# First loads of q and k cut by halves of 18-token rows, and a new order of all steps, in a fused window attention and expert attention kernel

## The chip, the cores and the metric

The kernel runs on one core of a Trainium2 chip. The core has a matrix engine (TensorE, PE in the profile), VectorE (DVE), ScalarE (ACT), GpSimd (POOL), and SyncE (SP), which here only issues transfers; 16 DMA engines move data between the memory of the chip (HBM) and the core's own memory. The metric is the time of one execution on the device, in microseconds (us); lower is better.

## The reference

Two layers follow each other. The first is attention over 576 tokens with a window of 32 to each side, for 8 batches and 8 heads of width 64. Its output, with the heads side by side, is the input of the second: four experts with causal attention, of which a gate picks two for each token.

```python
# first layer: q, k, v are (8, 8, 576, 64)
scores = (q @ k.T) / 8
scores = where(abs(i - j) <= 32, scores, -1e9)
x = softmax(scores) @ v                      # -> x: (8, 576, 512), heads side by side
# second layer
logits = x @ w_gate                          # 4 experts, the best 2 of each token
w = softmax(logits of the best 2)
for e in range(4):
    q, k, v = x @ wq[e], x @ wk[e], x @ wv[e]          # 64 wide
    ye = softmax(causal(q @ k.T / 8)) @ v @ wo[e]
    out += (w of expert e where chosen) * ye
```

## The kernel before

The whole kernel is a list of steps, `ORDER`, a long string. A loop at the end of the program goes through it and calls for each word the function of that name: the digits are arguments (the batch first), the digits behind `@` are banks of PSUM, the small memory into which TensorE writes, and a last letter `a`, `v` or `g` is the engine that does a copy or a mask (ScalarE, VectorE or GpSimd). Each engine works through its own instructions in the order in which the list issues them, and an instruction waits until its inputs have been written and its outputs are free. So the list alone sets what stands behind what on each engine, and one late instruction holds up all that is queued behind it on its engine.

For batch `b`, head group `g` (four heads each) and half `half` of the tokens, the steps are:

- `lq`, `lk`, `lv`: SP issues the loads of q, k and v. `load()` ties each to the last TensorE instruction that was issued before it in the list, so that loads don't run far ahead.
- `tq`, `tk` (function `turn`): VectorE turns q and k in blocks of 32 by 32, so that the head dimension lies on the partitions. A q or k tile holds 18 consecutive tokens of one head in each partition (4 heads by 32 partitions).
- `sc`: TensorE makes the scores of one half of the tokens; `ex`: ScalarE takes the exponential; `mk`: GpSimd, or in two cases VectorE, multiplies by the window's mask.
- `av`: TensorE multiplies by v and by a column of ones; `vc` copies parts of v to where `av` needs them; `un`: VectorE divides by the sums.
- `xt`, `xf`, `xb`: x is turned by TensorE, copied out of PSUM, and cast to bf16.
- `ga`, `gt`, `ge`, `gm`, `gu`: the gate and its top two.
- `pp`, `pe`, `pv`, `ve`, `ps`, `xe`, `se`, `po`, `oe`, `pt`, `ot`, `py`, `ye`, `st`: projections, causal attention of the experts, the output projection and the store, each product with the copy that takes it out of PSUM.
- `wl0` to `wl3` load the weights, `cw0` to `cw3` cast them to bf16. `s_pads` sets the padding of a dozen tiles to zero on VectorE, `s_ones` sets some ones, `s_mask` makes the mask on GpSimd, `s_warm` makes ScalarE load its table.

The q and k of batch 0 are loaded in halves, by steps of their own: `fk` (issued by SP) and `fq` (issued by ScalarE) call `first_load`, and `gk` and `gq` call `first_turn`. The half `x` of a head group is one range of tokens, so that each partition gets 9 (or 10 and 8) consecutive tokens of it, and the half of the scores that lies in that range can begin before the other half has been loaded. The source is written with the heads outermost: 4 heads, then 32 rows, then the elements of a row.

Of the kernel before, what the change touches and what calls it, by code (L numbers as in the profile page):

```python
# [20 lines left out]
HS = 288  # L21
# [8 lines left out]
    un03@6 un02@4 xt00@0 xt02@2 lv13 xt01@4 xf00@0v mk1001 mk1010 xb00@g cw1@v xf02@2a xf01@4a sc110@26  # L30
    xb02@g mk1011 xb01@v cw0@v lv14 lk21 sc111@04 ex1100@2 ex1110@0 ex1111@4 ga0@2 lv10 pp000@0 ex1101@6
    lv11 tq20 gt0@2 pp001@6 vc11@a ge0@2 pe000@0a gm0@2 gu0@2 tk20 pe001@6a pp011@4 pe011@4a lq31 pp010@0
    pe010@0a mk1000 mk1110 mk1111 ps002@4 xe002@4 ps000@2 wl2 av12@6 xe000@2 mk1100 mk1101 un12@6 av13@0
    ps003@4 vc10@g ps001@2 ps012@6 xe003@4 xe001@2 xe012@6 lq21 un13@0 av14@4 un14@4 xt11@0 wl3 xf11@0a
    ps013@4 ps010@2 av10@6 xe010@2 xe013@4 tk21 lq30 av11@0 un10@6 sc201@42 un11@0 lv23 ex2010@4 mk2010
    xt12@6 lk30 ex2011@2 xt10@0 cw2@v xf10@0a pv00@4 pv01@7 lv24 lv22 ve00@4a sc200@02 ex2000@0 se013 xb10@g
    se003 ex2001@2 lv33 xb11@g xf12@6v tq21 ve01@7v xb12@v se000 sc211@46 ex2111@6 mk2011 ex2110@4 mk2000
    se001 mk2001 ps011@0 xe011@0 pp111@2 pp100@6 pe111@2a lv32 sc210@04 ex2100@0 pe100@6a vc21@a lv21 lv20
    ga1@2 pv10@0 ex2101@4 lk31 ve10@0a po000@6 pp101@4 tq30 tk30 lq40 tq31 gt1@2 oe000@6 gm1@2 ge1@2
    pe101@4a pp110@0 pe110@0a cw3@a gu1@2 sc301@46 lv34 lq50 mk2110 se011 mk2111 mk2101 mk2100 av24@0  # L40
    ex3010@4 ex3011@6 av22@2 un24@0 ps112@0 ps100@6 un22@2 xe100@6 xe112@0 vc31@a vc20@g av23@4 un23@4
    av21@2 un21@2 lv41 lv31 av20@6 ps101@4 ps102@0 un20@6 xe101@4 xt21@2 xe102@0 xf21@2v se010 lv43 se101
    lv30 po010@6 xt22@4 xf22@4a xt20@0 xf20@0a xb22@v oe010@6 se100 xb21@g sc300@42 lk40 ga2@0 ex3000@4
    ex3001@2 tk31 xb20@g ps103@4 xe103@4 ps111@6 ps113@2 xe113@2 pt000@1 ot000@1v gt2@0 gm2@0 mk3011 xe111@6
    pv20@4 ge2@0 pt010@1 ot010@1v gu2@0 ve20@4a lv42 tq40 sc311@62 ex3110@6 ex3111@2 lk41 pp211@4 mk3010
    sc310@60 se113 mk3001 mk3000 pe211@4a ex3101@0 mk3110 se103 mk3101 ex3100@6 mk3100 mk3111 lv40 lq41
    pp201@4 py01@0 tk40 vc30@g pe201@4a pp200@6 pe200@6a sc401@42 ex4011@2 ex4010@4 lv44 ye01@0v st01
    sc400@60 ex4000@6 ex4001@0 tk41 av34@2 ps202@4 ps110@6 py02@3 xe202@4 xe110@6 av33@0 lk50 av31@4 un34@2
    pv11@2 ve11@2a vc40@g ye02@3a av30@6 tq41 un33@0 un31@4 un30@6 mk4000 mk4011 av32@0 un32@0 po100@4 lq51
    xt32@2 xt30@6 xf30@6a lq60 oe100@4 xf32@2v pp210@0 sc411@24 pe210@0a sc410@06 lk51 se111 tk50 vc41@g  # L50
    mk4010 se110 ex4110@2 ex4111@4 ps211@2 ex4100@0 xe211@2 ex4101@6 mk4110 tq50 xt31@4 py00@0 xf31@4v
    po110@2 oe110@2 ps212@4 ps213@6 ye00@0a xe213@6 xe212@4 mk4111 av43@0 se201 ps200@6 st00 xb32@g lv50
    un43@0 xb30@v xe200@6 ps201@2 st02 lv54 xe201@2 ga3@4 gt3@4 ge3@4 gm3@4 gu3@4 sc500@60 mk4100 mk4101
    mk4001 xb31@g av42@2 ex5001@0 ps210@0 ps203@4 un42@2 ex5000@6 lk60 xe203@4 xe210@0 pp300@6 pp301@2
    pt100@0 pt110@1 tk51 ot100@0v pe300@6a tq51 sc501@64 lk61 ot110@1a pe301@2a ex5010@6 ex5011@4 av44@0
    ps302@2 ps301@6 lq70 se210 mk5010 xe302@2 mk5011 se211 un44@0 pv31@1 se200 se203 mk5000 ve31@1a av40@4
    un40@4 py12@0 av41@2 pv21@1 un41@2 xe301@6 lv52 ye12@0a sc510@46 tk60 xt42@0 py10@2 ve21@1a ex5100@4
    ex5101@6 xf42@0v lv53 lv51 xt41@4 py11@6 ye10@2a se213 ye11@6v xf41@4a po210@2 xt40@4 xf40@4a pp310@6
    oe210@2 xb42@g ps303@2 xe303@2 pe310@6a ps300@0 st11 st10 po200@4 xb40@g xb41@v lv62 vc51@g xe300@0 lq61
    pt210@2 ot210@2v pp400@6 pe400@6v oe200@4 sc511@20 ex5111@0 ex5110@2 pp311@6 pe311@6v tq60 tq61 vc50@g  # L60
    se301 tk61 lv60 lv64 st12 lv63 mk5101 mk5111 mk5001 pp411@0 pt200@2 pe411@0a ot200@2a pp401@6 ps311@0
    pe401@6a ps312@4 pv30@2 xe311@0 xe312@4 sc601@06 ga4@4 ve30@2a ex6010@0 ex6011@6 ps400@0 ps403@2 mk5110
    mk5100 gt4@4 xe403@2 ps313@6 av54@5 xe313@6 vc61@g se303 lk70 sc600@62 ge4@4 xe400@0 gm4@4 gu4@4 un54@5
    av50@0 un50@0 ex6001@2 ex6000@6 ps310@2 ps402@4 av53@6 lv61 xe402@4 xe310@2 se403 se313 mk6000 se310
    un53@6 av52@0 un52@0 av51@4 py22@2 pv41@3 un51@4 ye22@2a ve41@3a sc610@06 sc611@24 ex6100@0 ex6101@6
    lv70 lk71 ex6111@4 ex6110@2 tq70 se300 xt50@0 py20@6 po300@2 xt51@4 mk6001 xf50@0a se311 tk70 py21@0
    xf51@4a oe300@2 ye20@6v mk6110 xb50@g mk6111 lq71 se401 pp410@2 pt300@4 xt52@5 st20 xf52@5a po310@6
    ot300@4v pv40@4 xb52@v oe310@6 ve40@4v xb51@g ye21@0a pe410@2a ps413@6 xe413@6 mk6011 ps412@2 ps401@0
    xe401@0 mk6010 se400 vc60@g xe412@2 se411 mk6100 mk6101 lv74 st21 pp510@6 pe510@6v tq71 pp501@4 pe501@4a
# [561 lines left out]
```

## Time and profile before

| | us |
|---|---|
| median of 3 runs | 280.54 |
| lowest and highest | 278.0 and 280.75 |
| the profiled execution | 280.03 |
| its span (first to last instruction) | 278.1 |
| TensorE busy | 221.1 |
| VectorE busy | 192.6 |
| ScalarE busy | 151.8 |
| GpSimd busy | 150.8 |

The profiled execution took 280.03 us, of which 278.14 us are the span that the trace covers; 1.9 us lie around it. It is 0.5 us under the median of the three runs. Busy times are sums over a program with different stages: each says how much of the span an engine worked, not which of them set the time at a given moment.

### The profile page before, as it was taken

The numbers are of one execution on the slowest core, as the hardware profiler recorded it, in microseconds if no ns is written. First come the engines' busy times: TensorE is split into PE (matmuls) and PEld (weight loads), VectorE is DVE, ScalarE is ACT, GpSimd is POOL, SyncE is SP. The second block draws the span as 40 slices with busy tenths as digits, with TensorE's granted clock in tenths as the row PEclk, the third lists the DMA queues.
The fourth block names the chain that finished last, engine by engine and source line by source line (L and its number), as shares of the span: only waits on it lengthen the run. The fifth ranks groups of instructions, "written<-read, shape, count | busy, mean of one in ns | idle before, by whom it ended". The sixth has DMA issues, their size and how long they took to land.

```text
span 278.1 us, 12345 instructions
## 1 busy us (share of the span) xinstructions
PE 221.1 (79%) x5536; PEld 178.7 (64%) x5536; DVE 192.6 (69%) x381; ACT 151.8 (55%) x234; POOL 150.8 (54%) x166
## 2 busy tenths in 40 slices
...
GB/s 54 156 126 105 203 192 173 173 115 229 157 277 114 209 181 172 130 220 158 246 166 175 177 248 168 90 86 169 167 60 42 123 89 2 2 172 10 146 173 189
DMA packets 55286, 40.65 MB, mean 146 GB/s; under 512 B 45249, under 2 KB 46273, under 8 KB 55233
## 3 DMA queue, kind: packets, MB, share of 16 engines
...
q10 hardware_dynamic: 608, 1.25, 1.3%
...
## 4 chain that ended last, share of the span: by engine, by line
PE 50%; DVE 25%; DMA 10%; issue 7%; ACT 4%; POOL 1%; SPq 1%; ACTq 0%; DVEq 0%; POOLq 0%
PE PS L170 43%; DMA kn<-in_k_dram 10%; PE PS L173 7%; DVE Tqn L287 5%; DVE Tkn L287 4%; DVE XTB L158 2%; DVE XN L380 2%; DVE OE L548 1%; DVE PS L446 1%; DVE ATE L212 1%; DMA out_dram<-Y 1%; DVE A L354 1%; ACT A L350 1%; ACT QKE L154 1%; DVE WQ L158 1%
## 5 line engine op out<-in xcount | busy, mean ns | idle before, releaser
L354 POOL TENSOR_TENSOR A<-A,MASKP 128x576 f32<-128x576 f32 x62 | 87.5, 1432 | 49.1 <-ACT A L350 49.1
L170 PE MATMUL PS<-Tqn,Tkn 32*64 32x128 f32 (+2 forms) x2560 | 50.3, 285 | 30.2 <-DVE Tqn L303 15.6
L170 PEld LDWEIGHTS PS<-Tqn,Tkn 32*64 32x64 f32 x2560 | 43.5, 146 | 37.0 <-DVE Tqn L303 15.7
L350 ACT ACTIVATE A<-PS 128x576 f32<-128x576 f32 x64 | 38.4, 650 | 47.0 <-PE PS L170 44.5
L520 ACT ACTIVATE ATE<-PS 128x1024 bf16<-128x1024 f32 (+1 forms) x64 | 50.9, 839 | 13.0 <-PE PS L170 12.3
L170 PE MATMUL PS<-V,A 128*64 128x65 f32 (+1 forms) x1280 | 42.7, 231 | 8.1 <-DMA V<-in_v_dram 3.7
L170 PEld LDWEIGHTS PS<-V,A 128*64 128x64 f32 (+1 forms) x1280 | 38.8, 139 | 12.6 <-DMA V<-in_v_dram 3.8
L527 POOL TENSOR_SCALAR_AFFINE_SELECT ATE<-ATE 128x512 bf16<-128x512 bf16 (+1 forms) x48 | 24.8, 531 | 34.2 <-ACT ATE L520 28.1
L287 DVE STREAM_TRANSPOSE Tqn<-qn 128x576 f32<-128x576 f32 x28 | 32.4, 1240 | 0.7 <-PE PS L170 0.7
L287 DVE STREAM_TRANSPOSE Tkn<-kn 128x576 f32<-128x576 f32 x28 | 32.5, 1238 | 0.0
L156 POOL CAST XTB<-XTF 128x1024 bf16<-128x1024 f32 (+1 forms) x20 | 14.8, 758 | 31.3 <-DVE XTF L158 21.6
L154 ACT COPY XTF<-PS 128x1024 f32<-128x1024 f32 (+1 forms) x18 | 13.4, 769 | 25.9 <-PE PS L173 25.7
L380 DVE TENSOR_TENSOR XN<-PS,RC 128x512 f32<-128x512 f32 x32 | 22.1, 692 | 1.2
L173 PE MATMUL PS<-ident,XN 128*128 128x128 f32 x144 | 21.0, 294 | 1.6 <-issue 1.2
L156 POOL COPY V<-V 64x1024 f32<-64x1024 f32 (+1 forms) x22 | 21.2, 963 | 1.3
L170 PE MATMUL PS<-WO,OTT 128*128 128x512 bf16 (+1 forms) x96 | 19.5, 346 | 2.2 <-ACT ATE L520 1.5
L170 PE MATMUL PS<-XTB,WQ 128*128 128x288 bf16 x128 | 18.6, 288 | 2.3 <-ACT QKE L154 2.3
L154 ACT CAST QKE<-PS 128x576 bf16<-128x576 f32 x24 | 15.1, 644 | 8.5 <-PE PS L170 8.5
L173 PEld LDWEIGHTS PS<-ident,XN 128*128 128x128 f32 x144 | 17.1, 150 | 3.8 <-issue 1.4
L170 PE MATMUL PS<-WV,XTB 128*128 128x256 bf16 (+1 forms) x192 | 18.6, 255 | 1.1 <-DVE XN L386 0.5
L170 PE MATMUL PS<-QKE 64*128 64x64 bf16 (+4 forms) x192 | 17.0, 283 | 1.5 <-DVE OE L548 1.2
L170 PEld LDWEIGHTS <-ATE 128*128 128x128 bf16 x480 | 16.5, 97 | 2.6 <-issue 1.1
...
## 6 DMA issues: line engine op xcount, KB each, us to landing
...
qn<-in_q_dram SPq DMA_DIRECT2D x14, 576.0 KB, 5.0
kn<-in_k_dram SPq DMA_DIRECT2D x14, 576.0 KB
...
```

The costliest lines, as they stand in the source:

```text
L154: nc.scalar.copy(o, i)
L156: nc.gpsimd.tensor_copy(o, i)
L158: nc.vector.tensor_copy(o, i)
L170: PACE[0] = nc.tensor.matmul(*args, **kw)
L173: PACE[0] = nc.tensor.transpose(*args)
L212: nc.vector.memset(t[:, 2048:3584], 0.0)
L287: nc.vector.transpose(T[:, dh, :].rearrange("q (p o) -> q o p", o=18), n_[:, :, 32 * dh:32 * dh + 32])
L350: nc.scalar.activation(a_part(b, g, half, p), two(b0)[:, :, 0:HS], EXP, scale=scale_att)
L354: (nc.gpsimd if eng == "g" else nc.vector).tensor_tensor(out=ap, in0=ap, in1=MASK[:, None, HS * half:HS * half + HS].to_broadcast([128, 2, ...
L380: nc.vector.tensor_tensor(out=XN[T // 2][:, T % 2, :].rearrange("p (g h d) -> p g h d", g=2, h=4), in0=u[:, :, :, 0:64], in1=rc[:, :, :, N ...
L520: nc.scalar.activation(A[:, at:at + 2 * step].rearrange("p (e x) -> p e x", e=2)[:, :, 0:w], two(b0)[:, :, 0:w], EXP, scale=scale_moe)
L527: nc.gpsimd.affine_select(ap, ap, pattern=[[0, n], [1, w]], compare_op=IS_GE, fill=0.0, base=64 * j if c == 3 else 0, channel_multiplier=-1)
```

## The change

Two things are changed. The first is how the q and k of batch 0 are loaded and turned. A half is now the first or the last 9 tokens of each row of 18, over all 128 rows of a head group, and the source is written with these 128 rows outermost. Every half thus holds tokens from the whole length, and both halves of q and of k of a group have to be turned before any scores of that group can begin. The second is the list: all its steps are the same in number and kind, but they stand in another order, with other banks and partly with another engine for a copy. The two long strings share no line; the first lines of each are shown.

```diff
 ORDER = """
-    s_mask fq00 gq00 fk10 fq10 s_ones gk10 fk11 fk00 gq10 s_warm fq11 fq01 lq10 fk01 gk00 sc010@02 lv02
-    sc000@46 ex0101@2 ex0000@4 ex0100@0 lv01 lk10 gk11 gq01 lv00 gk01 gq11 sc001@04 tq10 tk10 s_pads lv03
...
+    fk01 fq01 fk11 s_pads fk00 s_warm gq01 s_ones fq10 fq00 fq11 gk00 lv04 lv14 fk10 lv01 lk10 gk01 gq00
+    sc001@02 ex0010@0 ex0011@2 gk11 gq11 gq10 gk10 lv02 sc000@46 ex0000@4 ex0001@6 lq10 lv00 sc011@64 tk10
+    s_mask mk0001@g ex0111@4 tq10 lv03 sc010@20 ex0110@6 mk0011@g mk0110@g s_ident mk0111@v lk11 mk0010@v
...
-    FIRST = {"qn": ((0, 9), (9, 18)), "kn": ((0, 10), (10, 18))}
-
     def first_load(nm, src, q_, g, x):
-        o0, o1 = FIRST[nm][x]
         t = NAT[nm][g][:, :, :].rearrange("p o d -> p (o d)")
-        q_.dma_start(t[:, 64 * o0:64 * o1], src[0, 4 * g:4 * g + 4, 32 * o0:32 * o1].rearrange(
-            "h (p o) d -> h p (o d)", p=32))
+        q_.dma_start(t[:, HS * 2 * x:HS * 2 * (x + 1)],
+                     src[0, 4 * g:4 * g + 4].rearrange("h (p o) d -> (h p) (o d)", o=18)[:, HS * 2 * x:HS * 2 * (x + 1)])

     def first_turn(nm, g, x):
-        o0, o1 = FIRST[nm][x]
         for dh in range(2):
-            nc.vector.transpose(QKT[nm][g][:, dh, 32 * o0:32 * o1].rearrange("q (p o) -> q o p", p=32),
-                                NAT[nm][g][:, o0:o1, 32 * dh:32 * dh + 32])
+            nc.vector.transpose(QKT[nm][g][:, dh, :].rearrange("q (p o) -> q o p", o=18)[:, 9 * x:9 * x + 9, :],
+                                NAT[nm][g][:, 9 * x:9 * x + 9, 32 * dh:32 * dh + 32])
```

Over the whole list the copies change engines as follows: `cw` on ScalarE 1 before and 3 now; `pe` on ScalarE 24 and 18; the large `ve` on ScalarE 5 and 7, the small one 6 and 3; the large `xf` on ScalarE 12 and 14, the small one 3 and 6; the large `xb` on GpSimd 12 and 8 (the others on VectorE); the large `ye` on ScalarE 11 and 13, the small one 8 and 5.

SP's queue at the start of the program, before. `kn` and `qn` are the k and q tiles as loaded, `V` the v tiles; 128x1x640 is a half of 128 rows with 640 elements each.

```order
L297 DMA kn_69<-in_k_dram 128x1x640
L297 DMA kn_69<-in_k_dram 128x1x512
L297 DMA kn_68<-in_k_dram 128x1x640
L177 DMA qn_67<-in_q_dram 128x1152
L297 DMA kn_68<-in_k_dram 128x1x512
L177 DMA V_75<-in_v_dram 128x8x64 x2
L177 DMA kn_70<-in_k_dram 128x1152
```

The same place now.

```order
L294 DMA kn_68<-in_k_dram 128x576
L294 DMA kn_69<-in_k_dram 128x576
L294 DMA kn_68<-in_k_dram 128x576
L177 DMA V_75<-in_v_dram 64x8x64
L177 DMA V_76<-in_v_dram 64x8x64
L294 DMA kn_69<-in_k_dram 128x576
L177 DMA V_75<-in_v_dram 128x8x64
L177 DMA kn_70<-in_k_dram 128x1152
L177 DMA V_75<-in_v_dram 128x8x64
L177 DMA qn_67<-in_q_dram 128x1152
```

Both halves of k of group 0 (`kn_68`) now stand among the first three, and the q of batch 1 (`qn_67`) has moved from the fourth to the tenth place, behind the first loads and four loads of v.

VectorE's queue from the first turns of q and k to the first masks, before. `Tqn` and `Tkn` are the turned q and k, `A` the scores that are masked; the rows of L210 to L217 are `s_pads`.

```order
L303 STREAM_TRANSPOSE Tqn_72<-qn_66 128x9x32 x2
L287 STREAM_TRANSPOSE Tqn_71<-qn_67 128x18x32 x2
L287 STREAM_TRANSPOSE Tkn_73<-kn_70 128x18x32 x2
L210 MEMSET XTF_83 128x4x64
...
L212 MEMSET ATE_93 128x768
...
L217 MEMSET WG 128x128
L354 TENSOR_TENSOR A_78<-A_78,MASKP 128x2x288 x2
L287 STREAM_TRANSPOSE Tqn_72<-qn_65 128x18x32 x2
L287 STREAM_TRANSPOSE Tkn_74<-kn_68 128x18x32 x2
L379 RECIPROCAL RC_101<-PS_63 128x8
```

VectorE's queue now, from its beginning to the first division.

```order
L210 MEMSET XTF_83 128x4x64
...
L212 MEMSET ATE_93 128x768
...
L217 MEMSET WG 128x128
L299 STREAM_TRANSPOSE Tqn_71<-qn_65 128x9x32 x2
...
L299 STREAM_TRANSPOSE Tkn_73<-kn_68 128x9x32 x4
L299 STREAM_TRANSPOSE Tqn_71<-qn_65 128x9x32 x2
L299 STREAM_TRANSPOSE Tkn_74<-kn_69 128x9x32 x2
L299 STREAM_TRANSPOSE Tqn_72<-qn_66 128x9x32 x4
L299 STREAM_TRANSPOSE Tkn_74<-kn_69 128x9x32 x2
L287 STREAM_TRANSPOSE Tkn_73<-kn_70 128x18x32 x2
L287 STREAM_TRANSPOSE Tqn_71<-qn_67 128x18x32 x2
L350 TENSOR_TENSOR A_78<-A_78,MASKP 128x2x288
L350 TENSOR_TENSOR A_77<-A_77,MASKP 128x2x288
L287 STREAM_TRANSPOSE Tkn_74<-kn_68 128x18x32 x2
L375 RECIPROCAL RC_101<-PS_61 128x8
```

The memsets of `s_pads` have moved from behind the turns to the very front, the four half turns of group 0 stand ahead of those of group 1, and the first division (`un02`) now stands between the turn of k and that of q of batch 1's second group.

## Rows read from the trace of the kernel before

**Rows 1.** The page: the span, and each engine's busy time, share and instructions.

```profile
span 278.1 us, 12345 instructions
PE 221.1 (79%) x5536; PEld 178.7 (64%) x5536; DVE 192.6 (69%) x381; ACT 151.8 (55%) x234; POOL 150.8 (54%) x166
```

**Rows 2.** The chain that ended last, 0 to 70 us: start, duration, what.

```profile
2.35 21.99 DMA kn<-in_k_dram
...
28.12 5.07 DMA kn<-in_k_dram
...
37.24 0.26 DVE XTF L210
...
41.59 0.14 DVE WG L217
...
43.01 4.05 issue
```

**Rows 3.** By stretch: PE, PEld, DVE, ACT, POOL busy; granted clock, DMA share, GB/s.

```profile
10.00:11.00 1.00, 0.00 (x0) 0.00 (x0) 0.30 (x2) 0.00 (x0) 0.00 (x0) 1.00 1.01 325
...
22.00:23.00 1.00, 0.00 (x0) 0.00 (x0) 0.00 (x0) 0.00 (x0) 0.00 (x0) 1.00 0.27 107
```

**Rows 4.** The q tiles, 0 to 45 us: the one landing on record.

```profile
DMA to landing us min/median/max: 23.5/23.5/23.5
```

**Rows 5.** DMA issues over the whole span: count, KB each, median us to landing.

```profile
qn<-in_q_dram SPq DMA_DIRECT2D x14, 576.0 KB, 5.0
```

**Rows 6.** Timeline of TensorE: start, duration, instruction, idle time before it.

```profile
15.57 2.39 PE L170 MATMUL PS<-Tqn,Tkn 32*64 32x96 f32 x80 [15.57 <-DVE Tqn L303]
25.16 2.45 PE L170 MATMUL PS<-Tqn,Tkn 32*64 32x96 f32 x80 [7.20 <-DVE Tkn L303]
...
58.65 2.50 PE L170 MATMUL PS<-Tqn,Tkn 32*64 32x96 f32 x160
...
62.31 1.15 PE L170 MATMUL PS<-XTB,WQ 128*128 128x288 bf16 x8
```

**Rows 7.** Busy time of PE, PEld, DVE, ACT, POOL in two stages.

```profile
0.00:62.30 62.30, 29.34 (x850) 25.84 (x850) 37.92 (x65) 13.61 (x23) 21.66 (x29) 0.92 0.51 144
62.30:273.00 210.70, 191.71 (x4690) 152.83 (x4686) 154.70 (x317) 137.16 (x212) 129.10 (x138) 0.99 0.49 145
```

**Rows 8.** Groups of instructions by shape: count, busy us, mean ns, idle before.

```profile
L354 POOL TENSOR_TENSOR A<-A,MASKP 128x576 f32<-128x576 f32 x62 | 87.5, 1432 | 49.1 <-ACT A L350 49.1
...
L287 DVE STREAM_TRANSPOSE Tqn<-qn 128x576 f32<-128x576 f32 x28 | 32.4, 1240 | 0.7 <-PE PS L170 0.7
L380 DVE TENSOR_TENSOR XN<-PS,RC 128x512 f32<-128x512 f32 x32 | 22.1, 692 | 1.2
...
L379 DVE RECIPROCAL RC<-PS 128x8 f32<-128x8 f32 x32 | 6.4, 200 | 7.0 <-PE PS L170 5.5 <-ACT ATE L520 0.8
...
L354 DVE TENSOR_TENSOR A<-A,MASKP 128x576 f32<-128x576 f32 x2 | 6.2, 3115 | 0.0
...
L158 DVE COPY XTF<-PS 128x1024 f32<-128x1024 f32 x4 | 4.9, 1220 | 1.9 <-PE PS L173 1.9
L303 DVE STREAM_TRANSPOSE Tqn<-qn 128x288 f32<-128x288 f32 x8 | 4.8, 677 | 8.6 <-DMA qn<-in_q_dram 8.6
...
L158 DVE CAST XTB<-XTF 128x1024 bf16<-128x1024 f32 x4 | 4.3, 1083 | 1.4 <-ACT XTF L154 1.3
```

**Rows 9.** Busy time in shorter stretches, columns as in rows 3.

```profile
44.00:48.00 4.00, 0.33 (x18) 0.23 (x20) 4.00 (x3) 0.00 (x0) 2.52 (x2) 1.00 1.00 224
48.00:58.00 10.00, 7.60 (x109) 7.11 (x98) 8.88 (x15) 0.43 (x2) 0.00 (x0) 0.50 0.57 168
70.00:72.00 2.00, 2.00 (x40) 2.00 (x40) 1.06 (x1) 1.60 (x2) 1.25 (x2) 0.53 0.35 82
```

**Rows 10.** The score matmuls of 128 columns, at 36 to 42 us and at 88 to 92 us.

```profile
L170 PE MATMUL PS<-Tqn,Tkn 32*64 32x128 f32 x96 | 4.3, 423 | 0.0
...
L170 PE MATMUL PS<-Tqn,Tkn 32*64 32x128 f32 x48 | 1.1, 277 | 0.0
```

More of the change, by code (lines that the diff above doesn't have):

```diff
@@ L30 @@
[L30 to L69, printed above, removed]
@@ new lines @@
+    sc001@02 ex0010@0 ex0011@2 gk11 gq11 gq10 gk10 lv02 sc000@46 ex0000@4 ex0001@6 lq10 lv00 sc011@64 tk10
+    s_mask mk0001@g ex0111@4 tq10 lv03 sc010@20 ex0110@6 mk0011@g mk0110@g s_ident mk0111@v lk11 mk0010@v
+    lq11 sc100@64 wl0 ex0100@2 ex0101@0 mk0101@g vc01@a tk11 mk0000@g av02@0 un02@0 av03@2 ex1000@6 ex1001@4
+    un03@2 lv13 sc101@46 lv12 tq11 mk1000 mk0100@g vc00@a ex1011@6 xt01@2 ex1010@4 av01@6 un01@6 av00@4
+    cw0@a xf01@2a wl1 av04@0 sc111@26 ex1110@2 ex1111@6 un00@4 un04@0 xt00@4 lv11 lk20 xt02@0 xf02@0a
@@ new lines @@
+    xf00@4v xb00@v xb02@v sc110@26 vc11@a ga0@0 gt0@0 gm0@0 mk1010 mk1001 ex1100@2 mk1110 xb01@g mk1011
+    mk1111 cw1@a ex1101@6 lv10 lk21 ge0@0 mk1101 gu0@0 pp010@4 pp000@2 pp001@6 pe010@4a lq20 pp011@4
+    pe001@6a pe011@4a mk1100 wl2 av13@0 tk20 un13@0 av12@6 un12@6 pe000@2a ps003@2 xe003@2 ps002@4 av14@0
+    ps012@2 wl3 un14@0 xt11@6 xe002@4 ps013@0 vc10@g tq20 xe012@2 xe013@0 ps000@4 lq21 xf11@6a xe000@4
+    av11@2 un11@2 av10@0 xt12@6 xf12@6a cw2@a sc201@42 lv24 lk30 ex2011@2 un10@0 sc200@06 xt10@2 ex2010@4
@@ new lines @@
+    tk21 ex2000@0 ex2001@6 xb12@g pv00@4 ps001@6 xf10@2a lq30 tq21 ve00@4a sc210@20 se003 xb10@v cw3@v
+    xe001@6 lv21 ga1@4 se013 xb11@g ex2100@2 ex2101@0 tk30 ps010@6 pv01@5 lv22 lv20 mk2001 mk2000 se001
+    mk2011 sc211@02 xe010@6 pv10@6 ve01@5v gt1@4 ge1@4 gm1@4 gu1@4 lv31 lv23 ex2110@0 pp100@0 ve10@6a
+    ex2111@2 pp101@4 tq30 pe101@4v pp110@6 pe110@6v pe100@0a lv30 pp111@0 ps103@4 xe103@4 se000 lv32 lk31
+    ps011@2 xe011@2 pe111@0v se011 mk2100 mk2010 mk2101 vc20@g po000@6 ps113@0 xe113@0 ps111@4 mk2111 mk2110
@@ new lines @@
+    oe000@6 xe111@4 av21@2 vc21@a un21@2 av20@0 ps100@4 ps102@6 lq31 av24@2 pv11@3 xe100@4 xe102@6 un20@0
+    se113 se010 un24@2 av23@0 un23@0 vc30@g lk40 av22@4 ve11@3a ps101@2 xe101@2 lv44 un22@4 sc300@60
+    ex3000@6 ex3001@0 lv33 lv42 ps112@4 xe112@4 xt20@2 xf20@2a tk31 xt22@6 pt000@7 xf22@6v xt21@0 po010@4
+    xf21@0a lv34 lq41 mk3000 ot000@7v sc301@26 tq31 ga2@0 mk3001 oe010@4 lq40 ex3011@6 ex3010@2 ps110@6
+    xe110@6 sc311@42 xb21@g se100 xb20@v tk40 gt2@0 xb22@g ex3110@4 se111 se101 ex3111@2 pt010@1 se103
```

67 lines of the change are left out of this document (44 added, 23 removed).

## The prediction

> **What bounds the kernel now.** I read the busy times first: TensorE works 221.1 of 278.1 us, the others much less [rows 1]. That average hides two stages. Up to 62.3 us TensorE is busy for 29.3 us, from there to 273 us for 191.7 of 210.7, which is 91% [rows 7]. The second stage is bound by TensorE and has 19 us of gaps; the first loses 33 us. The place that parts them is the first projection matmul, at 62.31 us [rows 6]. It is a good mark for both kernels, because in both lists TensorE has the same work ahead of it: eight score blocks, five `av`, three `xt` and one `ga`. I call it M and ask only two things: when M comes, and how long the rest takes (278.1 - 62.3 = 215.8 us now).
>
> The chain of waits says what fills the time to M. It holds one load of k from 2.35 us for 21.99 us, then another for 5.07 us, and on VectorE the memsets of `s_pads` from 37.24 to 41.73 us and a stop of 4.05 us inside the second mask [rows 2]. So loads come first, then VectorE.
>
> Why the first loads are slow is seen in the DMA share. At 22 us, with only first loads under way, the 16 DMA engines are busy to 0.27 and move 107 GB/s; at 10 us, when an ordinary load of q runs beside them, the share is 1.01 and 325 GB/s [rows 3]. A quarter of the engines carry the first loads. The eight of them are 4 x (128 rows x 18 x 64 x 4 bytes) = 2.36 MB, and 2.36 MB at 107 GB/s is 22.1 us, which is the length of that wait. What queues behind them suffers too: a q load of 576 KB issued there took 23.5 us to land [rows 4], where 5.0 is the median [rows 5].
>
> The Trainium skill (DMA: Bandwidth & Descriptors, Why a DMA increments its semaphore by 16 and not by 1) states that a transfer issued from SP or ACT uses the largest number up to 16 that divides the slowest dimension of size above one. With heads outermost that is 4, and the share of 0.27 agrees; with 128 rows outermost it is 16.
>
> **The change part by part: the first loads.** The new form is that of the ordinary loads, only with shorter rows, so I give it their rate, some 300 GB/s (325 in the best stretch). Before the first scores now stand four loads, not two. Ahead of the last of them, `fk00` and `fq00`, lie `fk01`, `fq01`, `fk11` and `fq10`: six loads of 295 KB, 1.77 MB, 5.9 us from 2.35 us, so 8.3 us. VectorE then does three half turns, two instructions of 0.677 us each [rows 8], 4.1 us: first scores at about 12.5 us instead of 15.57 [rows 6]. That is a small gain; the larger is that nothing follows like the gap to the second block at 25.16 us, since group 1 lands right behind.
>
> **The change: VectorE's order.** `s_pads` takes 4.5 us and moves to the front, where VectorE waits for the first landing anyway; its cover is that wait of 7 to 8 us, and if it were gone it would cost 4.5 us. The work that is left up to M I sum along VectorE, which I take as the bound. Four half turns of group 1: 5.4 us, to 17.9. `tk10`: 2 x 1.24 = 2.5, to 20.4. `tq10` needs its load: it is tied to the end of `sc000`, second block, 12.5 + 2 x 2.4 = 17.3 us, and lands 5.0 us later at 22.3; turned at 24.8. Two masks: 6.2 us together as measured [rows 8], or 2.2 without the stop of 4.05: 27.0 to 31.0. `tk11` and `tq11`, 5.0; five divisions of 0.69 + 0.20, 4.5; `xf00`, 1.2; `xb00`, 1.1, and `xb02`, a smaller cast for which I take no more than that [rows 8]: 12.9 us, to 39.9 or 43.9. The last score block and the gate come in beside that, so M falls at 39.9 to 43.9 us if no engine waits for another in between.
>
> Does another engine come later? TensorE: at the upper clock a score block takes 1.25 us (two in 2.50), at the start 2.4 [rows 6]. The matmuls of 128 columns took 423 ns up to 42 us and 277 ns later [rows 10], so I read the start as the lower level (1.2 GHz), though the record shows no event there. Eight blocks, two of them at 2.4 us, are 12.3 us. The `av`, `xt` and `ga` are at most what is left of the 29.3 us [rows 7] when the score blocks are taken off (six of 2.4 and two of 1.25, 16.9 us): 12.4 us. From 12.5 us TensorE could reach M at 37 us. GpSimd: eleven masks of 1.43 us [rows 8] and the identity are some 16.5 us from about 18, so 35 us, and one cast. ScalarE, busy 13.6 us up to M now [rows 7], gets `cw0` and `cw1` besides, which VectorE loses. None is later than VectorE.
>
> The other end of the range for M is what one gets if only the loads improve and all waits after them stay. From the second block at 25.16 us, when nearly all first loads are in, to M the kernel now takes 37.1 us. From the second block of the new list, at 15 us, that gives 52 us, a lead of 10. The sum along VectorE gives a lead of 18 to 22. I take M at 45 us, a lead of 17: near the VectorE sum, since `s_pads` leaves the path for certain (4.5 us), but with a few us for waits between engines that the sum of one engine doesn't show.
>
> **The change: the rest of the list.** After M the work of every kind is the same. Copies change engines: by the counts given with the diff, at 0.3 to 1.2 us for such a copy [rows 8], ScalarE gains about 5 us, VectorE and GpSimd lose about 4 each. With 137 to 155 us busy out of 210.7 [rows 7] none of them is near the bound, so I cost this at nothing, covered by TensorE's 191.7 us. Just after M the old kernel has a pile-up on VectorE, and the clock falls to the lower level for some us (0.53 granted at 70 to 72 us [rows 9]); the new list has the weight casts on ScalarE there. I take 2 us off for it, 0 to 5 as bounds. Gaps otherwise: 19 us now, and another list may have 14 or 24; I take the same. The store at the end comes in the same steps.
>
> Sum: 278.1 - 17 - 2 = 259 us of span, and with the 1.9 us around it 261 us. The profiled execution is 0.5 us under the median, so I leave it at 261.
>
> **Rivals.** *First, the two masks on VectorE stay shut out.* Of the two now, one stood still for 4.05 us [rows 2] beside GpSimd's masks. In the new list GpSimd has eleven masks nearly in a row there. If each VectorE mask stops so, the two take 10.3 us, VectorE passes them at 35, M falls at 48, and TensorE, idle meanwhile, falls to the lower clock as it did after 48 us, when it had been idle for most of 4 us (0.50 granted up to 58 us [rows 9]): 3 us more, or up to 6 if GpSimd's runs are longer. Lead 8 to 11, total 267 to 270 us. For it: the same pair of steps in the same neighbourhood. Against it: GpSimd has to wait for `ex0100` and `ex0101` about then, which opens the door. The Trainium skill (SBUF — State Buffer, Who interferes with whom) states that a VectorE instruction with two inputs in that memory and a GpSimd instruction that reads it shut each other out, the earlier one to its end; the stop of 4.05 us agrees. Chance 0.2.
>
> *Second, the rest gets better as well.* If half of the 19 us of gaps after M go, the total is about 252 us. Nothing in the trace says that they would, apart from 0.99 granted clock and engines with room. Chance 0.12.
>
> *Third, slower than before.* The mechanism is a late instruction on ScalarE's queue. It takes all `ex` and `xe`, and now more `xf`, `ye` and the weight casts; where one stands ahead of an exponential that TensorE needs, TensorE stops, and long stops bring the lower clock, as the one before 48 us did for the 10 us that followed [rows 9]. One such stop costs some 3 us itself and 4 more by the clock (half of the 7.6 us that TensorE worked in those 10). It takes a gain of 19 us away with three of them and makes the kernel slower by over 1% from the fourth: 283 to 290 us. Against it: after M there is hardly one such stretch now. Chance 0.04.
>
> *Fourth, the new form doesn't spread over the DMA engines.* Then four loads come before the first scores, with two more mixed in, 1.77 MB at 107 GB/s, 16.5 us: first scores at 23 us, M at about 55.5, total 271. Chance 0.03.
>
> **How the numbers follow.** Forecast (255 to 267 us): 0.59, the four rivals 0.2, 0.12, 0.04 and 0.03, and 0.02 for a gain that several small losses use up. Predicted time 261 us. The range holds the forecast, half of the second rival, the first and the fourth: 251 to 272 us. Low end: lead 22 and 5 us off the rest is 253, and a little of the second rival; high end: lead 10 and nothing off is 270. A measurement of this kernel tells about 1% from no change, 2.8 us. Faster by over 1% hold forecast, first, second and fourth: with something taken off for what I can't see, 0.9; within 1% 0.05; slower 0.05.
>
> **What the new profile would show.** Right: a DMA share near 1 and 250 GB/s or more between 3 and 10 us; first scores at 11 to 14 us and the second block right behind; `s_pads` done by 6 us; the first projection matmul at 40 to 50 us; from there to the end 210 to 216 us, with TensorE near 91% busy. The first rival shows as VectorE masks of 5 us and more and a clock of 0.5 near 30 to 40 us. The prediction is wrong if M comes after 52 us, or if TensorE's busy share after M is under 87%, which would mean that the new list itself, not the loads, decides.

## The result, and the profile after

The changed kernel takes 264.74 us (median of 4 runs, 261.44 to 267.74), the kernel before 279.68 us beside it: a ratio of 0.943, 95% interval 0.932 to 0.954. The forecast was 261 us. A ratio, here and below, goes by the faster executions of both kernels alone, since some run one or more per cent longer at a lower granted clock, and so it is not the quotient of the medians. The profiled execution took 264.93 us, 263.2 us of it span.

The page of the changed kernel: the span, and each engine's busy time, share and instructions.

```profile
span 263.2 us, 12340 instructions
PE 217.3 (83%) x5523; PEld 173.8 (66%) x5536; DVE 186.4 (71%) x381; ACT 155.2 (59%) x236; POOL 149.0 (57%) x164
```

TensorE has the same 5536 matmuls as before [rows 1]. 13 of their records are missing here, all of `py` products with 512 columns. The changed kernel run again, below, has every record and nearly the same busy share after M, so the missing ones change little.

By stretch, the changed kernel (busy time of PE, PEld, DVE, ACT, POOL; granted clock, DMA share, GB/s):

```profile
3.00:4.00 1.00, 0.00 (x0) 0.00 (x0) 0.89 (x2) 0.00 (x0) 0.88 (x3) 1.00 1.03 396
6.00:7.00 1.00, 0.00 (x0) 0.00 (x0) 0.92 (x5) 0.00 (x0) 0.00 (x0) 1.00 1.05 411
...
39.00:258.50 219.50, 193.77 (x4669) 153.48 (x4682) 155.08 (x319) 135.69 (x207) 126.81 (x138) 0.98 0.49 143
87.00:91.00 4.00, 3.78 (x17) 2.13 (x17) 3.02 (x10) 1.89 (x4) 4.00 (x5) 0.57 0.49 146
88.00:89.00 1.00, 1.00 (x6) 0.63 (x5) 0.62 (x4) 0.54 (x2) 1.00 (x2) 0.50 0.54 55
207.00:211.00 4.00, 3.92 (x21) 2.61 (x20) 0.76 (x1) 2.08 (x4) 2.33 (x2) 0.57 0.34 131
246.00:248.00 2.00, 2.00 (x11) 1.44 (x10) 0.00 (x0) 0.97 (x2) 0.64 (x1) 0.50 0.18 47
```

The first two rows answer to [rows 3]: all 16 DMA engines carry the first loads, at 396 to 411 GB/s instead of 107. The third answers to the second stage of [rows 7]: TensorE is busy for 193.77 of 219.5 us, 88%, where it was 91%. The last four rows are from three stretches of a low granted clock after M. A mean of 0.57 over four us is 0.50, the lower level (1.2 GHz), for more than three of them. Inside these stretches TensorE works nearly without a gap, but each lies directly behind a stop of TensorE or begins in one: of 2.07 us, of 1.81 and 0.88 us, and of 2.45 us (rows below).

The chain of waits of the changed kernel, from its start (start, duration, what):

```profile
1.72 5.96 DMA kn<-in_k_dram
7.70 2.34 DVE Tkn L299 x4
10.04 0.55 DVE Tqn L299
10.64 4.45 PE PS L170 x139
```

Where one load of k held the chain for 21.99 us [rows 2], loads now hold it for 6 us. Next, TensorE's timeline (start, duration, instruction, idle time before it and what ended it) at the places that answer to [rows 6], and at five later ones:

```profile
10.64 4.44 PE L170 MATMUL PS<-Tqn,Tkn 32*64 32x64 f32 x160 [10.64 <-DVE Tqn L299]
16.36 3.70 PE L170 MATMUL PS<-Tqn,Tkn 32*64 32x64 f32 x160 [1.28 <-ACT A L346]
...
39.03 0.65 PE L170 MATMUL PS<-XTB,WQ 128*128 128x288 bf16 x4 [0.70 <-DVE XTB L158]
40.40 1.64 PE L170 MATMUL PS<-XTB,WQ 128*128 128x288 bf16 x12 [0.72 <-DVE XTB L158]
...
86.28 0.44 PE L173 MATMUL PS<-ident_bf,OE 128*128 128x128 bf16 x5 [2.07 <-DVE PS L445]
...
132.41 1.62 PE L170 MATMUL PS<-V,A 128*64 128x65 f32 x49 [2.35 <-issue]
...
147.11 0.45 PE L173 MATMUL PS<-ident_bf,OE 128*128 128x128 bf16 x5 [2.75 <-DVE G L464]
...
205.18 1.02 PE L170 MATMUL PS<-WO,OTT 128*128 128x512 bf16 x3 [1.81 <-ACT A L346]
...
245.00 0.64 PE L170 MATMUL PS<-WO,OTT 128*64 128x256 bf16 x4 [2.45 <-DVE G L464]
```

M, the first projection matmul (the mark that the prediction chose), comes at 39.03 us instead of 62.31: a lead of 23.3 us. But only 14.9 us of it reach the end of the span, since the rest of the program takes 224.2 us instead of 215.8. Three of the later rows have one cause. They are the first steps `pt010`, `pt200` and `py52`, and each waits for a step of the gate (`gt`, L445, or `gu`, L464). Gate waits are not new: by the view of waits TensorE lost 4.1 us to gate steps after M before (2.7 behind `ge`, 1.2 behind `gt`, 0.2 behind `gu`); now it is 7.3 us, in three long ones.

The two masks on VectorE, [rows 8], in VectorE's timeline now:

```profile
21.40 1.50 DVE L350 TENSOR_TENSOR A<-A,MASKP 128x576 f32<-128x576 f32 x2
```

1.50 us for both, where it was 6.2. One of the two is another step than before: VectorE had `mk0110` and `mk0111` and now has `mk0111` and `mk0010`, of the same shape.

### The profile page after: what moved, and what is told of

It reads as the page before. It is cut to its first block, busy times and chain, and to the rows that moved or that the text cites. A ratio compares the mean times of both kernels' runs of the same rounds, so it can differ in the third digit from the quotient of the medians.

```text
span 263.2 us, 12340 instructions
## 1 busy us (share of the span) xinstructions
PE 217.3 (83%) x5523; PEld 173.8 (66%) x5536; DVE 186.4 (71%) x381; ACT 155.2 (59%) x236; POOL 149.0 (57%) x164
## 4 chain that ended last, share of the span: by engine, by line
PE 73%; DVE 12%; issue 6%; ACT 5%; DMA 4%; SPq 0%; DVEq 0%; ACTq 0%
PE PS L170 65%; PE PS L173 8%; DVE XTB L158 2%; DMA kn<-in_k_dram 2%; DMA V<-in_v_dram 1%; ACT Y L154 1%; ACT A L346 1%; ACT ATE L516 1%; DVE Tkn L299 1%; DVE Tkn L287 1%; DVE Y L158 1%; DVE PS L442 1%; ACT OTT L154 1%; DVE OTT L158 1%; DVE XTF L158 0%
## 5 line engine op out<-in xcount | busy, mean ns | idle before, releaser
L170 PE MATMUL PS<-Tqn,Tkn 32*64 32x128 f32 (+2 forms) x2560 | 46.4, 275 | 14.5 <-DVE Tqn L299 10.6
L170 PEld LDWEIGHTS PS<-Tqn,Tkn 32*64 32x64 f32 x2560 | 40.9, 140 | 18.8 <-DVE Tqn L299 10.8
L170 PE MATMUL PS<-V,A 128*64 128x65 f32 (+1 forms) x1280 | 40.0, 222 | 7.3 <-issue 3.1
L170 PEld LDWEIGHTS PS<-V,A 128*64 128x64 f32 (+1 forms) x1280 | 36.3, 131 | 11.5 <-issue 4.8
L376 DVE TENSOR_TENSOR XN<-PS,RC 128x512 f32<-128x512 f32 x32 | 22.1, 692 | 1.2
L154 ACT COPY XTF<-PS 128x1024 f32<-128x1024 f32 (+1 forms) x26 | 16.6, 676 | 8.0 <-PE PS L173 5.2
L170 PE MATMUL PS<-WV,XTB 128*128 128x256 bf16 (+1 forms) x192 | 20.0, 264 | 0.7 <-ACT ATE L516 0.4
L154 ACT COPY Y<-PS 128x1024 f32<-128x1024 f32 (+1 forms) x18 | 15.0, 839 | 8.0 <-PE PS L170 7.4
L170 PE MATMUL PS<-XTB,WK 128*128 128x288 bf16 x128 | 19.6, 300 | 0.0
L156 POOL CAST XTB<-XTF 128x128 bf16<-128x128 f32 (+1 forms) x18 | 10.9, 622 | 13.3 <-ACT XTF L154 12.7
L173 PEld LDWEIGHTS PS<-ident,XN 128*128 128x128 f32 x144 | 15.6, 140 | 4.0 <-issue 2.7
```

Source lines behind the costliest of these rows:

```text
L154: nc.scalar.copy(o, i)
L156: nc.gpsimd.tensor_copy(o, i)
L170: PACE[0] = nc.tensor.matmul(*args, **kw)
L173: PACE[0] = nc.tensor.transpose(*args)
L376: nc.vector.tensor_tensor(out=XN[T // 2][:, T % 2, :].rearrange("p (g h d) -> p g h d", g=2, h=4), in0=u[:, :, :, 0:64], in1=rc[:, :, :, N ...
```

## The experiments

I split each kernel at M and write "rest" for span minus M. Ratios are against the kernel before, run beside each experiment.

### The changed kernel again, and the two halves of the change crossed

Theory: the loads and the new order up to M give the lead, the new order after M takes part of it back. Rival: the loads are all of the gain, and the new list does nothing.

The changed kernel once more, nothing edited.

> The changed kernel once more, as the reference for the three others on the same chip: 262 to 266 us, first projection matmul at 39 us and 222 to 225 us after it. If the three long stops of TensorE behind the gate (2.1, 2.8 and 2.5 us in the first trace) belong to the list and not to that one execution, they stand here again with the same sizes.

265.5 us, ratio 0.959 (0.949 to 0.968), M at 40.62, rest 224.0. Its stretch after M, with all records, and its timeline of TensorE at the places shown above:

```profile
40.62:259.90 219.28, 194.65 (x4682) 153.65 (x4682) 154.61 (x319) 134.25 (x205) 125.59 (x137) 0.98 0.49 142
```

```profile
82.78 1.14 PE L170 MATMUL PS<-Tqn,Tkn 32*64 32x64 f32 x63 [1.49 <-issue]
...
131.84 1.62 PE L170 MATMUL PS<-V,A 128*64 128x65 f32 x49 [2.08 <-issue]
...
146.55 0.45 PE L173 MATMUL PS<-ident_bf,OE 128*128 128x128 bf16 x5 [2.76 <-DVE G L464]
...
246.39 0.64 PE L170 MATMUL PS<-WO,OTT 128*64 128x256 bf16 x4 [2.45 <-DVE G L464]
```

The second and third gate waits stand again to 0.01 us, and a stop near 132 us without a known cause as well. Ahead of `pt010` there is no gate wait; the time went by in other stops just ahead of it. The gate waits thus come to 5.2 us here, and the rest is the same. TensorE is busy for 89% of the stretch after M, with 24.6 us of gaps. The clock falls in three stretches again (from 147, 208 and 246 us, 0.57 over four us each), each at a stop of 1.8 to 2.8 us.

The old list with the new loads. Both halves must be turned before any scores of a group, so two pairs of turns go ahead of the scores:

```diff
-    ... gk00 sc010@02 lv02
-    sc000@46 ex0101@2 ex0000@4 ex0100@0 lv01 lk10 gk11 gq01 lv00 gk01 gq11 sc001@04 ...
+    ... gk00 gk11 gq11 sc010@02
+    lv02 gk01 gq01 sc000@46 ex0101@2 ex0000@4 ex0100@0 lv01 lk10 lv00 sc001@04 ...
```

> The list of before with the new form of the first loads; the only steps moved are the second half turns of each group, which now have to stand ahead of that group's first scores. My theory: the loads alone are worth about 10 us (the gap of 7.2 us before the second score block goes, s_pads stays where it was on VectorE, and the rest of the list costs its old 216 us after the first projection matmul, which falls at about 52 us): 268 to 272 us. Rival (the loads are all of the gain, the list none): 261 to 266 us. Rival (the gain is the list's): 277 us or more.

264.29 us, ratio 0.946 (0.936 to 0.956). Two rows of TensorE's timeline, the first scores and M:

```profile
12.20 4.53 PE L170 MATMUL PS<-Tqn,Tkn 32*64 32x96 f32 x160 [12.20 <-DVE Tqn L299]
...
45.94 1.15 PE L170 MATMUL PS<-XTB,WQ 128*128 128x288 bf16 x8
```

The lead is 16.4 us where I expected about 10, and the rest, 261.6 - 45.94 = 215.7 us, is that of before. In time the loads alone give all that the whole change gives. My expectation missed.

The new list with the old loads (the old `first_load` and `first_turn` put back):

> The new list with the old form of the first loads (heads outermost, contiguous halves). My theory: four slow loads stand before the first scores, at 107 GB/s, so these begin at about 20 us, the first projection matmul falls at 49 to 53 us, and the new list's rest costs its 224 us: 273 to 279 us. Rival (the list alone gives the gain, the loads are hidden): 262 to 268 us.

281.98 us, ratio 1.013 (1.005 to 1.021): the new list without the new loads is about 1% slower than the kernel before. First scores at 24.46 us, because group 0 now needs all its quarters; M at 57.12, rest 222.9.

The new list up to the first gate, then the old order, with the new loads (the steps that are left over stand in the old list's order):

```diff
     ... ga0@0 gt0@0 gm0@0 ... ge0@0 mk1101 gu0@0
-    (the new list's further steps)
+    (the same steps in the order of the old list)
```

> The new list up to the end of the first gate, then all that is left in the order of the old list; new loads. In the changed kernel the first projection matmul comes at 39 us and the rest takes 224 us, in the one before 62 and 216. My theory, that the rest of the new list is the worse one by itself: first projection matmul at 39 to 41 us, then 216 us, 255 to 260 us in all. Rival, that the rest takes longer because it starts earlier (loads crowd, the clock falls): 262 to 267 us, with 222 to 226 us after that matmul.

261.77 us, ratio 0.940 (0.933 to 0.947). M was at 43.15 and not 39 to 41, since at the seam of the lists `pp000` waits 4.93 us for the first gate; the rest takes 215.5 us. The rest came as expected, the time (255 to 260 us) was missed by that wait.

The counterpart: the old list up to the first gate's `ga`, then the new order, with the new loads.

> The old list up to the first gate with the new loads (second half turns ahead of the scores), then all that is left in the order of the new list. My theory: the first projection matmul falls where it does in the old list with the new loads, at about 50 to 53 us, and the rest takes 224 us: 275 to 279 us. Rival, that the start decides how long the rest takes: 216 to 218 us of rest, 267 to 272 us.

275.99 us (median of ten), ratio 0.982 (0.976 to 0.988); M at 48.97, rest 225.4. This execution's span, 274.4 us at a mean clock of 0.947, is 3 to 5 us longer than those behind the ratio (269.1 to 271.3), and its M and rest together are too long by as much.

Together, the rest by list and start:

| | first loads | list up to M | M | old rest | new rest |
|---|---|---|---|---|---|
| before | old | old | 62.31 | 215.8 | |
| list alone | old | new | 57.12 | | 222.9 |
| loads alone | new | old | 45.94 | 215.7 | |
| crossed | new | new | 43.15 | 215.5 | |
| crossed | new | old | 48.97 | | 225.4 |
| changed | new | new | 39.03, 40.62 | | 224.2, 224.0 |

The rest goes by its own list, whatever comes before it: 215.5 to 215.8 us with the old order (215.7 to 216.4 in the later runs that keep it whole), 223 to 224 with the new, and 225.4 in the execution at the low clock. The theory holds, and the rival holds only for the net time: the new front gives 5 to 7 us more than the loads alone, and the new rest loses 8.

I tried another seam, behind `pe011`, to get the new front and the old rest without the 4.93 us.

```diff
     ... pe011@4a
-    (the new list's further steps)
+    (the same steps in the order of the old list)
```

> As the run with the new front and the old rest, but the cut lies behind the first four projections and copies, so that none of them waits for the bank in which the first gate works (a stop of 4.9 us in that run). Theory: first projection matmul at 39 us as in the changed kernel, 216 us after it: 256 to 258 us, the fastest so far. Rival (that stop only hid others): 260 to 262 us.

265.15 us, ratio 0.958 (0.950 to 0.966), a miss: M at 40.80, rest 221.7. VectorE's timeline and TensorE's show the new seam:

```profile
47.91 2.34 DVE L287 STREAM_TRANSPOSE Tqn<-qn 128x576 f32<-128x576 f32 x2 [4.18 <-DMA qn<-in_q_dram]
```

```profile
53.21 0.39 PE L170 MATMUL PS<-QKE 64*128 64x320 bf16 x4 [4.08 <-DVE XN L376]
```

The new front issues the load `lq20` late, and the old order turns its tile (`tq20`) soon after the cut: that holds up VectorE's queue for 4.18 us, and TensorE 4.08 us later on. Lists cut in the middle don't fit each other. The old order takes its 215.5 us only where its loads have been issued in time, and this run tells nothing more about the rest.

### What makes the first loads slow

Rival to "heads outermost": a short row makes a load slow. In the kernel before each first load is written as four, one for each head, so that rows keep their length and 32 rows are outermost:

```diff
-        q_.dma_start(t[:, 64 * o0:64 * o1], src[0, 4 * g:4 * g + 4, 32 * o0:32 * o1].rearrange(
-            "h (p o) d -> h p (o d)", p=32))
+        for h in range(4):
+            q_.dma_start(t[32 * h:32 * h + 32, 64 * o0:64 * o1],
+                         src[0, 4 * g + h, 32 * o0:32 * o1].rearrange("(p o) d -> p (o d)", p=32))
```

> The kernel before, its list and its contiguous halves, with each first load written as four loads, one of each head, so that 32 rows are outermost; the same bytes in the same places. Theory (heads outermost is what keeps the first loads on a quarter of the DMA engines, the 18-token rows matter little): loads spread, no stretch at a share of 0.25, first projection matmul at 46 to 50 us, 264 to 270 us, a little lost to the issue of 32 loads instead of 8. Rival (the long contiguous rows of 18 tokens are what helps): 275 to 282 us.

268.71 us, ratio 0.955 (0.943 to 0.968). By stretch, as above:

```profile
3.00:4.00 1.00, 0.00 (x0) 0.00 (x0) 0.00 (x0) 0.00 (x0) 0.88 (x3) 1.00 0.97 243
5.00:6.00 1.00, 0.00 (x0) 0.00 (x0) 0.01 (x1) 0.00 (x0) 0.00 (x0) 1.00 0.64 178
...
9.00:10.00 1.00, 0.09 (x8) 0.09 (x12) 1.00 (x3) 0.00 (x0) 0.00 (x0) 1.00 0.90 190
11.00:12.00 1.00, 1.00 (x57) 1.00 (x44) 1.00 (x2) 0.00 (x0) 0.00 (x0) 1.00 1.01 361
```

The same tokens, the same rows: with the head out of the outermost place the share is 0.64 to 1.04 in each us from 2 to 13 us, and M comes at 49.20, 13.1 us sooner. The number of loads under way doesn't explain it: before, seven of the eight first loads had been issued by 4.7 us, and the share from 5 to 9 us was 0.25 to 0.26. The outermost dimension is the cause of the low share. That M is 3.3 us later than with the new form (45.94) goes with a lower rate, 178 to 361 GB/s, and with the issuing: the last of the 32 loads is issued at 13.7 us, the last of the eight of the new form at 5.3. The run doesn't separate the two.

### What the new front gives beside the loads

Theory: `s_pads` in front is most of it. The old list with the new loads, and `s_pads` moved to its start:

```diff
-    s_mask fq00 gq00 fk10 fq10 ... sc001@04 tq10 tk10 s_pads lv03
+    s_pads s_mask fq00 gq00 fk10 fq10 ... sc001@04 tq10 tk10 lv03
```

> The list of before with the new loads, and the padding memsets moved to the front of VectorE's queue; nothing else. Theory: their 4.5 us stand on the path to the first projection matmul when they follow the turns, and lie under the first landing when they lead, so that matmul moves from 45.9 to 41 to 42 us and the whole from 264 to 259 to 261 us. Rival (VectorE has room there once the loads are fast): no change, 263 to 265 us.

259.04 us, ratio 0.934 (0.924 to 0.945); M at 41.73, rest 215.7. The expectation held: 4.2 us of M, of the 4.5 that `s_pads` takes. The rest of the new front is worth 1 to 3 us. These two edits of the old list, the loads and the place of `s_pads`, are 6.5 us faster than the whole change beside them (265.5 us).

### What the new rest loses

Theory: the gate works inside one bank of PSUM, in a tile that spans two banks, and a TensorE step that writes the other bank of this tile waits for all gate steps that the list has issued before it. Three times the new list has the gate steps first: `gt2` (bank 0) then `pt010` (bank 1); `gt4` to `gu4` (bank 0) then `pt200` (bank 1); `gt7` to `gu7` (bank 6) then `py52` (bank 7). VectorE's timeline in the changed kernel, ahead of `pt200`, shows how long that is:

```profile
142.22 0.37 DVE L442 STREAM_TRANSPOSE PS<-PS 128x160 f32<-128x160 f32 x1 [0.51 <-PE PS L170]
...
143.69 0.18 DVE L456 TENSOR_TENSOR PK<-PS,m 128x20 f32<-128x20 f32 x1
143.79 1.37 DVE L158 CAST XTB<-XTF 128x128 bf16<-128x128 f32 x2
145.08 1.21 DVE L158 COPY Y<-PS 128x1024 f32<-128x1024 f32 x1
146.21 0.17 DVE L461 TENSOR_TENSOR PS<-PS,PK 128x20 f32<-128x20 f32 x1
...
146.86 0.20 DVE L464 TENSOR_TENSOR G<-PS,su 128x20 f32<-128x20 f32 x1
```

The gate's own steps are short, but two casts and a copy of 2.4 us stand between `gm4` (to L456) and `gu4` (from L461), and `pt200` starts at 147.11, right behind the last of them. Rival: the old rest is better in many small places, and these waits cover one another.

The changed kernel with the three TensorE steps ahead of the gate steps, nothing else moved:

```diff
-    ... tk40 gt2@0 xb22@g ex3110@4 se111 se101 ex3111@2 pt010@1 se103
+    ... tk40 pt010@1 gt2@0 xb22@g ex3110@4 se111 se101 ex3111@2 se103
-    ... sc511@46 gt4@0 gm4@0 ... ex5111@6 lv63 pt200@1 se311
+    ... sc511@46 pt200@1 gt4@0 gm4@0 ... ex5111@6 lv63 se311
-    gt7@6 gm7@6 ge7@6 gu7@6 ps700@4 py52@7 ye52@7a
+    py52@7 gt7@6 gm7@6 ge7@6 gu7@6 ps700@4 ye52@7a
```

> The changed kernel with three steps of TensorE moved in the list ahead of the gate's VectorE steps that they now wait for (pt010 ahead of gt2, pt200 ahead of gt4, py52 ahead of gt7). They write the other half of the PSUM tile in which the gate works. My theory: the wait is for that shared tile, it stops TensorE for 2.1, 2.8 and 2.5 us and is most of the 8 us by which the new rest is longer; without it 257 to 261 us. Rival (TensorE stops there anyway, for the next thing that VectorE brings late): 262 to 266 us.

256.99 us (256.65 to 257.59), ratio 0.928 (0.918 to 0.938): 8.5 us less than the same kernel without the edit beside it. Its page, and the places where the changed kernel stood still or ran at a low clock:

```profile
span 255.9 us, 12353 instructions
PE 215.3 (84%) x5536; PEld 173.8 (68%) x5536; DVE 185.3 (72%) x381; ACT 154.8 (60%) x236; POOL 149.0 (58%) x164
```

```profile
40.40:251.00 210.60, 191.64 (x4682) 153.18 (x4682) 153.18 (x319) 134.21 (x205) 125.56 (x137) 0.99 0.51 148
85.00:89.00 4.00, 3.96 (x74) 3.10 (x75) 2.67 (x9) 2.43 (x4) 3.94 (x4) 1.00 0.61 173
...
200.00:208.00 8.00, 6.27 (x149) 4.71 (x150) 2.75 (x11) 6.76 (x11) 4.75 (x4) 1.00 0.17 66
242.00:246.00 4.00, 4.00 (x73) 3.69 (x72) 2.90 (x11) 1.45 (x3) 0.88 (x2) 0.57 0.74 272
```

TensorE's timeline at three places, two of them those of the first two gate waits:

```profile
85.04 1.04 PE L170 MATMUL PS<-Tqn,Tkn 32*64 32x128 f32 x49 [0.98 <-issue]
...
128.63 1.67 PE L170 MATMUL PS<-V,A 128*64 128x65 f32 x49 [0.24 <-issue]
...
142.70 1.91 PE L170 MATMUL PS<-WV,XTB 128*128 128x256 bf16 x16 [1.79 <-ACT A L346]
```

M at 40.37 and rest 215.5 us, the old rest to a few tenths, with TensorE at 91% again. The edit of the three steps gives back all that the new rest had lost, 8.5 to 8.7 us. Not all of that is the 7.3 us of the three waits themselves. Of these, 3.5 us stay as other stops near the same places: 0.98 and 1.79 us in the rows above, the second behind an exponential on ScalarE, and 0.72 at 241.03. So the rival holds in part: a gate wait had covered other waits. Another 2.1 us is the stop near 132 us, 2.35 in the changed kernel and 0.24 here at the same matmuls (128.63); why it goes with the edit is not shown. The remaining 2 to 3 us are busy time, 191.64 us where the same work took 193.77 and 194.65: each of those traces has three stretches of the lower clock after M, this one has one (242 to 246 us). The old rest has gate waits too, 4.1 us of them. Since the gaps after M are 19.0 us both before and here, apart from the gate the new rest must stand still some 4 us longer than the old, and its gain without gate waits only makes it equal. For the stretch at 207 us, 60 us behind a gate wait, the run shows only that the low clock went as well (1.00 from 200 to 208 us); the two stops just before it, 1.81 and 0.88 us on ScalarE's scores and copies, are in both traces (1.80 and 0.87).

Is it the tile, or the moved step? The changed kernel with `py52` in a bank of another tile, nothing moved:

```diff
-    gt7@6 gm7@6 ge7@6 gu7@6 ps700@4 py52@7 ye52@7a xe700@4 pv70@2
+    gt7@6 gm7@6 ge7@6 gu7@6 ps700@4 py52@3 ye52@3a xe700@4 pv70@2
```

> The changed kernel with one step's bank changed and no step moved: py52 and its copy ye52 use bank 3 instead of bank 7, which is the other half of the tile in which the last gate works (bank 6). Theory (the wait is for the shared tile): TensorE's stop of 2.45 us ahead of py52 goes or falls under 1 us, 262 to 264 us beside 265. Rival (it waits because of its place in the list, or VectorE is late anyway): the stop of 2.4 to 2.5 us stands, 264 to 266 us.

261.9 us, ratio 0.940 (0.930 to 0.949). TensorE's timeline:

```profile
241.23 0.61 PE L170 MATMUL PS<-QKE 64*128 64x448 bf16 x6
241.88 0.41 PE L170 MATMUL PS<-WO,OTT 128*64 128x256 bf16 x4
243.78 1.91 PE L170 MATMUL PS<-WV,XTB 128*128 128x256 bf16 x16 [1.49 <-ACT Y L154]
```

`py52` follows its predecessor at once: the stop of 2.45 us was the tile's. For the two other steps this was not tried by itself. 1.49 us come back one step later, since `ye52` now holds the tile in which `pv70` (bank 2) writes. The time is 2.8 us under the changed kernel's median of the first comparison, more than the 1 us net, and within what two runs of it differ by; the ratios are 0.940 here and 0.943 and 0.959 there. It is the stop, not the time, that answers the question.

### Two attempts at more

The old list with new loads and `s_pads` first also has gate waits, the longest 1.00 and 1.75 us, both behind `ge`. Moving its steps in the same way:

```diff
-    ... gt2@0 ... pt010@1 ...   ... gt6@4 ... pt410@5 ...
+    ... pt010@1 gt2@0 ...       ... ga6@4 pt410@5 gt6@4 ...
```

> The list of before with the new loads and the padding memsets first, and besides pt010 moved ahead of gt2 and pt410 ahead of gt6, the two places where that list has TensorE wait for a gate in the same tile (1.00 and 1.75 us). Theory: 1.5 to 2.7 us off the 259.0 us of the run without this, so 256 to 258 us. Rival: the stops reappear at the next step, 258 to 260 us.

259.82 us, ratio 0.930 (0.921 to 0.939): the two waits are gone and no time is gained. The trace has stops of another kind instead:

```profile
30.47 0.31 PE L170 MATMUL PS<-Tqn,Tkn 32*64 32x64 f32 x1 [2.54 <-issue]
...
160.96 2.61 PE L170 MATMUL PS<-V,A 128*64 128x65 f32 x82 [1.65 <-issue]
```

In these rows TensorE waited for nothing that the profile shows, so the run settles nothing on what two shorter waits are worth.

And the version without gate waits, with the exponentials `ge` and the `gu` of two batches later in the list, behind ScalarE work that TensorE needs sooner:

```diff
+    ... gt6@6 gm6@6 ex7111@2 pe601@0a ge6@6 gu6@6 py30@2 ...
+    ... ye10@2v ex5110@4 ex5111@6 ge4@0 gu4@0 ...
```

> The version without the three gate waits (257.0 us), and besides the gate's exponential of batches 4 and 6 moved behind the two exponentials of scores that it now precedes on ScalarE; the stops there are 1.8 us each (TensorE waits for the bank that the scores leave). Theory: 1.5 to 3.5 us off, 253.5 to 255.5 us. Rival (the gate's result is then late in its turn): 256 to 258 us.

258.31 us, ratio 0.926 (0.917 to 0.933): no gain, a miss. TensorE's timeline has two new stops near the moved steps:

```profile
144.99 2.10 PE L170 MATMUL PS<-XTB,WQ 128*128 128x288 bf16 x8 [2.70 <-DVE Y L158]
...
204.83 0.44 PE L173 MATMUL PS<-ident_bf,OE 128*128 128x128 bf16 x5 [2.84 <-ACT OTT L154]
```

A step that is moved out of one engine's way is in another's. The version with the three steps ahead of the gate stays the fastest of those timed by its median, 257 us; by the ratios, 0.928 and 0.926, the two can't be told apart.

## Why the prediction was right, and where it was wrong

261 us stood against 264.7, within the range, but two of its terms were off by more, in opposite directions: M by 6.0 us (45 taken, 39.0 measured) and the rest by 10.4 (213.8 taken, 224.2 measured). That the sum came out within 4 us is luck in that measure.

**The DMA engines.** Right in kind and small in size. A share near 1 was foreseen and measured (1.03 to 1.05), at 396 to 411 GB/s rather than the 300 that I took from the best stretch of before [rows 3]. First scores were forecast for 12.5 us and came at 10.64. The fourth rival, loads that don't spread, is false. One reading was too neat: the 22.1 us of all eight loads at 107 GB/s is not the one wait of 21.99 us, since VectorE waited for the last two of them until 27.2 and 29.9 us.

**M, mis-sized.** I set it at 45 us between a sum along VectorE (39.9 to 43.9) and an end of 52 "if only the loads improve and all waits after them stay". The sum was the better guide: 39.03 and 40.62 us. The other end was wrong in itself. The loads alone gave M at 45.94, because the waits after the second block did not stay: from there to M it took 27.9 us (18.01 to 45.94 in the trace of the loads alone), not 37.1. Part of those waits had themselves come from late loads. `s_pads` was priced at 4.5 us and gave 4.2; it had to be taken off after the loads, not held as part of a compromise. Two readings on the other engines were off without weight: ten masks of GpSimd, not eleven, stand ahead of the cast that M needs, and GpSimd's busy time after M was 129 us, below the 137 to 155 that I gave.

**The first rival, the masks on VectorE.** The mechanism depends on where GpSimd's masks lie, as I said; GpSimd has no mask from 21.37 to 23.02 us, and VectorE's two, not the same pair of steps as I wrote, take 1.50 us there, so the rival did not occur. With the loads alone the old pair took 3.9 us.

**The rest, the step that failed.** "Gaps otherwise: 19 us now, another list may have 14 or 24; I take the same", with 2 us taken off for the pile-up after M. The window after M has 25.7 us without a TensorE record, 24.6 in the repeat, and 2 to 3 us more of busy time, since the clock falls in three stretches instead of one. Three steps of the new list stand behind gate steps whose bank shares a tile with theirs, at 7.3 us (5.2 in the repeat) where the old list lost 4.1 to gate steps; a stop of 2.1 to 2.4 us near 132 us comes on top. I counted the copies that change engines, and no cost of theirs shows: with the three waits removed the same copies give a rest of 215.5 us. What I did not read was the new order's banks: `gt4@0` ahead of `pt200@1` can be seen in the list. The second rival, a better rest, is false in sign; the third, slower by late instructions on ScalarE, did not occur, though stops with the lower clock did come: one such stretch stands behind stops that ScalarE ended, two behind VectorE's gate steps.

**The marks.** Bandwidth, `s_pads` (done by 5.5 us) and the share after M (88%, against 87% as the mark for "the list itself decides") fell as set out. First scores, at 10.64, and M, at 39.03, came just ahead of their marks, and the rest, at 224.2, beyond its 210 to 216. With its share just above the line the mark let the list pass, although the list takes back 8 us of the 23.

**Open.** TensorE's stop near 132 us, for which the profile shows no cause, stood at the same matmuls in all five traces of the new order with the gate steps first (2.35, 2.08, 2.35 with the other tile, 2.90 with the old loads, 2.90 with the old front) and is 0.24 and 0.26 us in the two versions with the three steps moved. So it goes with that edit; by what way, nothing here tells.
